# A gated recurrence with an FFT long convolution: gate factors made in float32r inside the scan, one batch ahead, and the filter's spectrum read from DRAM

## The chip, the cores and the metric

The kernel runs on one core of a Trainium2 chip. The metric is the device time of one execution in microseconds (us). TensorE (PE) multiplies, VectorE (DVE) and ScalarE (ACT) move and combine data, GpSimd (POOL) does elementwise work on SBUF, and SyncE (SP) issues the DMAs from one queue in order. Every engine runs its own instructions in their order and waits on semaphores for the others.

## The reference, cut to what matters

`B = 4`, `S = 6272`, `D = 256`. Two layers follow each other:

```python
sig = 1.0 / (1.0 + np.exp(-f_logit))
f = lower_bound + (1.0 - lower_bound) * sig
for t in range(S):                       # a gated scan over the sequence
    h = f[:, t] * h + (1 - f[:, t]) * x[:, t]
    y[:, t] = h
proj = y @ w_proj                        # 256 -> 768
x1, x2, x3 = proj[..., :D], proj[..., D:2*D], proj[..., 2*D:]
X2 = rfft(x2, n=S, axis=1); H = rfft(filter_fft, n=S, axis=0)
x2_conv = irfft(X2 * H, n=S, axis=1)     # circular convolution along the sequence
out = (x1 * x2_conv * x3) @ w_out
```

The length 6272 is split as 128 x 49, so that both transforms are matrix products.

## The kernel before, in words

For every batch `b` these stages follow each other:

- `hgrn(b)`: 13 chunks of 512 positions (the last has 128). A chunk loads `xt` and `ft` (512 KB each, `hg` pool, three buffers), takes the sigmoid on ACT (L139), multiplies on POOL (L140), and then, for each half `kh` of the 256 channels: four PE transposes of `ft` into bank 6 of PSUM (L146), four of `xt` into bank 7 (L148), an ACT pass that makes `fT` (L150) and the scan on DVE (L153). The scan reads bank 7 and writes the state as float16 into `HA`. Bank 6 and bank 7 have one copy each, so the second half's transposes wait for the first half's readers.
- `wraps()`: six DMAs inside `HA` that lay the state out periodically.
- `phase_p(b)`, `phase_f1(b)`: the product with the middle third of `w_proj` and the first transform; the result `A` overwrites the middle of `HA`.
- `mini(b)` and `units(b)`: 16 units. A unit makes two products of a transform matrix with `A` (L449, PSUM banks 0 and 1), multiplies each on DVE with the filter's spectrum `H`, which stays in SBUF (L453, into `PP`), transforms back with 16 products (L461, banks 2 and 3) and copies the result to `Th` on ACT (L464).
- `phase_z(b)`: 13 groups of 490 positions, each in two halves `jb`. For a half, `x1` (bank 4) and `x3` (bank 5) are made from `HA` with four float16 matmuls each (L408: two halves of the channels, each with the weight's high part `W13h` and its low part `W13l`); ACT scales `x1` into `x1s` (L413), DVE multiplies both into `z` (L414). Both inputs of L414 are read in the order `r m`, with a step of 49 floats, and `z` lies as `[.., r, m]`.
- `phase_o(b)`: 13 steps: 16 last products of the inverse transform (L481), DVE multiplies by `z` in place (L485), 16 products with `w_out` (L493), ACT copy (L497), DMA out.

In the main loop `units(b)`, `phase_z(b)` and `hgrn(b+1)` are stepped together; the last batch has only the first two. Before the loop, `prepare` (tables, weights, and the filter's transform) is woven with `hgrn(0)`: it rearranges the filter into a high part `f2h` (ACT, L316) and a low part `f2l` (DVE, L317), transforms it with three float16 matmuls for each of 128 column blocks (L325 to L327), and then per group of 8 blocks with four float32r matmuls of 512 columns (L338), whose result ACT writes to `H` (L340). `pair()` hands out four pairs of PSUM banks in turn.

The order of the instructions on each engine is not this program order: a scheduler sorts them by priority and by when it expects them to be ready, and the pools decide where waits for free buffers stand.

## Time and profile before

| what | value |
|---|---|
| time, median of 3 runs | 833.88 us (832.01 to 840.72) |
| the profiled execution's own time | 831.66 us |
| its span, first to last instruction | 830.0 us |
| PE busy, of the span | 697.1 us (84%) |
| DVE busy | 554.7 us (67%) |
| ACT busy | 400.5 us (48%) |
| POOL busy | 141.3 us (17%) |
| chain that ended last: PE, DVE, DMA | 39%, 23%, 10% of the span |

Busy PE time counts each matmul from its start to its modelled end, and matmuls overlap: a row `366` ns long may stand 0.21 us behind the one before it. So the start-to-start distance of rows says what PE work costs, and the busy sum does not. A row "x4" merges four instructions; the last number in brackets is idle time of the engine before the row, with what ended it.

### The profile page before, as it was taken

The numbers are of one execution on the slowest core, as the hardware profiler recorded it, in microseconds if no ns is written. First come the engines' busy times: TensorE is split into PE (matmuls) and PEld (weight loads), VectorE is DVE, ScalarE is ACT, GpSimd is POOL, SyncE is SP. The second block draws the span as 40 slices with busy tenths as digits, with TensorE's granted clock in tenths as the row PEclk, the third lists the DMA queues.
The fourth block names the chain that finished last, engine by engine and source line by source line (L and its number), as shares of the span: only waits on it lengthen the run. The fifth ranks groups of instructions, "written<-read, shape, count | busy, mean of one in ns | idle before, by whom it ended". The sixth has DMA issues, their size and how long they took to land.

```text
span 830.0 us, 14314 instructions
## 1 busy us (share of the span) xinstructions
PE 697.1 (84%) x5924; PEld 498.0 (60%) x5924; DVE 554.7 (67%) x587; ACT 400.5 (48%) x498; POOL 141.3 (17%) x157
## 2 busy tenths in 40 slices
...
GB/s 327 248 117 175 152 65 203 2 1 103 154 125 152 179 216 160 1 51 118 160 130 116 251 204 58 1 102 155 124 153 85 155 162 1 1 1 1 1 121 191
DMA packets 64672, 97.99 MB, mean 118 GB/s; under 512 B 3296, under 2 KB 54368, under 8 KB 63840
## 3 DMA queue, kind: packets, MB, share of 16 engines
...
## 4 chain that ended last, share of the span: by engine, by line
PE 39%; DVE 23%; DMA 10%; issue 8%; ACT 5%; POOL 1%; DVEq 0%; ACTq 0%; SPq 0%; POOLq 0%
PE PS L493 11%; DVE PP L453 8%; PE PS L461 8%; DMA ft<-in_f_logit_dram 7%; PE PS L408 7%; DVE z L414 6%; PE PS L369 5%; DVE z L485 4%; DVE HA L153 4%; PE PS L481 2%; ACT x1s L413 2%; DMA xt<-in_x_dram 2%; PE PS L146 2%; PE PS L148 1%; PE PS L384 1%
## 5 line engine op out<-in xcount | busy, mean ns | idle before, releaser
L408 PE MATMUL PS<-HA,W13h 128*128 128x490 f16 (+1 forms) x416 | 152.3, 366 | 17.6 <-DVE z L414 17.4
L408 PE MATMUL PS<-HA,W13l 128*128 128x490 f16 (+1 forms) x416 | 152.3, 366 | 0.0
L414 DVE TENSOR_TENSOR z<-PS,x1s 128x490 f16<-128x490 f32 (+1 forms) x104 | 100.7, 968 | 75.7 <-ACT x1s L413 38.0
L140 POOL TENSOR_TENSOR xt<-xt,ft 128x1024 f32<-128x1024 f32 (+1 forms) x52 | 116.4, 2238 | 204.0 <-DMA xt<-in_x_dram 115.7
L453 DVE TENSOR_TENSOR PP<-PS,H 98x1008 f16<-98x1008 f32 x128 | 149.2, 1197 | 1.9 <-PE PS L449 1.7
L153 DVE TENSOR_TENSOR_SCAN HA<-fT,HA,PS 128x512 f16<-128x512 f32 (+1 forms) x96 | 116.0, 1208 | 50.2 <-PE PS L148 29.8
L461 PEld LDWEIGHTS <-PP 98*128 98x128 f16 x1024 | 83.8, 97 | 71.7 <-issue 47.0
L150 ACT ACTIVATE fT<-PS,nomc 128x512 f32<-128x512 f32 (+1 forms) x104 | 68.8, 661 | 104.4 <-PE PS L146 55.9
L485 DVE TENSOR_TENSOR z<-PS,z 128x1024 f16<-128x1024 f32 (+1 forms) x52 | 58.2, 1158 | 87.5 <-PE PS L481 87.5
L493 PE MATMUL PS<-Woh,z 128*128 128x256 f16 x392 | 89.0, 276 | 21.6 <-DVE z L485 21.6
L461 PE MATMUL PS<-VB,PP 98*128 98x196 f16 x512 | 95.7, 248 | 3.7 <-DVE PP L453 3.6
L493 PEld LDWEIGHTS <-z 128*128 128x128 f16 x784 | 75.2, 99 | 35.2 <-DVE z L485 25.9
L464 ACT CAST Th<-PS 128x784 f16<-128x784 f32 x64 | 52.0, 812 | 77.1 <-PE PS L461 77.1
L497 ACT ACTIVATE osb<-PS 128x1024 f32<-128x1024 f32 (+1 forms) x52 | 50.4, 973 | 80.1 <-PE PS L493 73.4
L493 PE MATMUL PS<-Wol,z 128*128 128x256 f16 x392 | 88.6, 276 | 0.0
L413 ACT ACTIVATE x1s<-PS 128x490 f32<-128x490 f32 (+1 forms) x104 | 59.2, 569 | 51.9 <-PE PS L408 51.8
L139 ACT ACTIVATE ft<-ft 128x1024 f32<-128x1024 f32 (+1 forms) x52 | 52.7, 1014 | 63.0 <-DMA ft<-in_f_logit_dram 62.5
L461 PE MATMUL PS<-VA,PP 98*128 98x196 f16 x256 | 58.7, 246 | 27.0 <-DVE PP L453 25.0
...
L146 PE MATMUL PS<-iden,ft 128*128 128x128 f32 x392 | 63.7, 281 | 18.1 <-ACT ft L139 11.4
L148 PE MATMUL PS<-iden,xt 128*128 128x128 f32 x392 | 65.3, 288 | 13.0 <-DVE HA L153 6.7
L408 PEld LDWEIGHTS <-W13l 128*128 128x128 f16 x416 | 40.5, 97 | 58.3 <-issue 29.1
(120 smaller groups left out, 971.3 us busy)
## 6 DMA issues: line engine op xcount, KB each, us to landing
xt<-in_x_dram SPq DMA_DIRECT2D x48, 512.0 KB, 4.8
ft<-in_f_logit_dram SPq DMA_DIRECT2D x48, 512.0 KB, 3.9
out_dram<-osb SPq DMA_DIRECT2D x48, 512.0 KB, 2.6
...
HA<-HA SPq DMA_DIRECT2D x12, 512.0 KB, 5.1
...
```

The costliest lines, as they stand in the source:

```text
L140: nc.gpsimd.tensor_tensor(xt[:, 0:nb], xt[:, 0:nb], ft[:, 0:nb], op=AOP.mult)
L146: nc.tensor.transpose(sT[:, j * 128:(j + 1) * 128], ft[:, j, cols], iden[:])
L148: nc.tensor.transpose(uT[:, j * 128:(j + 1) * 128], xt[:, j, cols], iden[:])
L150: nc.scalar.activation(fT[:, 0:n], sT, AF.Identity, scale=nomc[:, kh:kh + 1], bias=1.0)
L153: nc.vector.tensor_tensor_scan(HA[:, h0:h0 + n], fT[:, 0:n], uT, 0.0 if c == 0 else HA[:, h0 - 1:h0], op0=AOP.mult, op1=AOP.add)
L408: nc.tensor.matmul(PS[:, 4 + i, 0:cn], w[:, kh, js], HA[:, h0:h0 + cn], start=(n == 0), stop=(n == 3))
L413: nc.scalar.activation(x1s[:, 0:cn], PS[:, 4, 0:cn], AF.Copy, scale=ZS)
L414: nc.vector.tensor_tensor(z[:, jb, :, m0:m0 + mn], PS[:, 5, 0:cn].rearrange("p (m r) -> p r m", r=Q), x1s[:, 0:cn].rearrange("p (m r) -> p ...
L453: nc.vector.tensor_tensor(P[:TB, o, :, :, 1:64], px.unsqueeze(1).broadcast_to([TB, 2, UE, 63]), hh, op=AOP.mult)
L461: nc.tensor.matmul(o, P[:TB, a, h, 2 * pr:2 * pr + 2, :], v[:TB], start=(n == 0), stop=(n == 3))
L485: nc.vector.tensor_tensor(zz, pc[:, :, 0:rn * 128].rearrange("p a (i m) -> p a i m", m=128), zz, op=AOP.mult)
L493: nc.tensor.matmul(po[:, i, :], z[:, kh, r0 + i, :], w[:, kh, :], start=(n == 0), stop=(n == 3))
```

## The change

- `phase_z` is gone. In `hgrn`, after both scans of a chunk, `x1` and `x3` of that chunk are made with `W13` in float32r (eight matmuls of up to 512 columns, new L164, instead of 16 of 490), still in banks 4 and 5, with `x1s` (new L167, one buffer) and the product `z` (new L168) in position order. `z` has two buffers, since it is now made while the batch before is still in use.
- The scan (still L153) writes a float32r tile `h` (two buffers for each half); a POOL copy (L158) puts it into `HA` as float16.
- `units` no longer finds `H` in SBUF: `prepare` writes it to 16 DRAM tiles (L350), and each unit loads its piece `Hu` (196 KB, two buffers) by a DMA on SP's queue (L431) and multiplies with it (L439).
- `phase_o` reads `z` at a step of 49 elements (98 bytes) and writes the product to a new tile `y` inside `PP` (L473).
- In `prepare` the filter is one float32r tile `f2` (copied by ACT and DVE in turn, L325 and L327) and transformed with one float32r matmul of 128 columns for each block (L334) instead of three; weights are loaded first, `pair()` uses two pairs of banks until `prepare` has ended.
- `units(b)` and `hgrn(b+1)` are woven evenly; the last batch has `units` alone.

```diff
@@ hgrn
+                h = hg.tile([128, CH], F32R, name="h", tag=f"h{kh}")
                 nc.vector.tensor_tensor_scan(
-                    HA[:, h0:h0 + n], fT[:, 0:n], uT,
-                    0.0 if c == 0 else HA[:, h0 - 1:h0], op0=AOP.mult, op1=AOP.add)
+                    h[:, 0:n], fT[:, 0:n], uT,
+                    0.0 if c == 0 else last[kh][:, CH - 1:CH].bitcast(F32),
+                    op0=AOP.mult, op1=AOP.add)
+                last[kh] = h
+                nc.gpsimd.tensor_copy(HA[:, HB[kh] + t0:HB[kh] + t0 + n],
+                                      h[:, 0:n].bitcast(F32))
+            for jb in range(2):
+                for i in range(2):
+                    js = slice(i * 256 + jb * 128, i * 256 + jb * 128 + 128)
+                    for kh in range(2):
+                        nc.tensor.matmul(PS[:, 4 + i, 0:n], W13[:, kh, js], last[kh][:, 0:n],
+                                         start=(kh == 0), stop=(kh == 1))
+                x1s = hg.tile([128, CH], F32, name="x1s", tag="x1s", bufs=1)
+                nc.scalar.activation(x1s[:, 0:n], PS[:, 4, 0:n], AF.Copy, scale=ZS)
+                nc.vector.tensor_tensor(z[:, jb, t0:t0 + n], PS[:, 5, 0:n], x1s[:, 0:n],
+                                        op=AOP.mult)
             yield
@@ prepare
-            nc.scalar.copy(dh, src)
-            nc.vector.tensor_tensor(dl, src, dh, op=AOP.subtract)
+            if r0 % 8:
+                nc.vector.tensor_copy(fv[:, :, :, r0:r0 + rn], src)
+            else:
+                nc.scalar.copy(fv[:, :, :, r0:r0 + rn], src)
...
-                nc.tensor.matmul(pa[:, i, :], f2h[:, cs], D1[:], start=True, stop=False)
-                nc.tensor.matmul(pa[:, i, :], f2l[:, cs], D1[:], start=False, stop=False)
-                nc.tensor.matmul(pa[:, i, :], f2h[:, cs], D1l[:], start=False, stop=True)
+                nc.tensor.matmul(pa[:TB, i, :], f2[:, c0:c0 + TB], D1r[:],
+                                 start=True, stop=True)
...
-            nc.scalar.activation(H[:TB, :, u, :], px[:TB], AF.Copy, scale=HS)
+            hw = hws[u % 4]
+            nc.scalar.activation(hw[:TB], px[:TB], AF.Copy, scale=HS)
+            nc.sync.dma_start(H[u][:], hw[:TB])
@@ units
+            Hu = cw.tile([128, 2, UE * 64], F16, name="Hu", tag="Hu")
+            nc.sync.dma_start(Hu[:TB], H[u][:])
...
-                hh = H[:TB, :, u, :].rearrange("p a (i k) -> p a i k", k=64)[:, :, :, 1:64]
+                hh = Hu[:TB].rearrange("p a (i k) -> p a i k", k=64)[:, :, :, 1:64]
@@ phase_o
+        z = zt[b % 2][:].rearrange("p k (m r) -> p k r m", r=Q)
...
-            zz = z[:, :, r0:r0 + rn, :]
+            y = PP[:, r0 // 4 % 4 // 2, r0 // 4 % 2].rearrange(
+                "p a i k -> p a (i k)").rearrange("p a (i m) -> p a i m", m=128)[:, :, 0:rn]
             nc.vector.tensor_tensor(
-                zz, pc[:, :, 0:rn * 128].rearrange("p a (i m) -> p a i m", m=128), zz,
-                op=AOP.mult)
+                y, pc[:, :, 0:rn * 128].rearrange("p a (i m) -> p a i m", m=128),
+                z[:, :, r0:r0 + rn, :], op=AOP.mult)
@@ main loop
-        gu, gz = units(b), phase_z(b)
-        gh = hgrn(b + 1) if b + 1 < B else iter(())
-        for step in range(NU):
-            next(gz, None)
-            next(gu)
-            if step >= 2:
-                next(gh, None)
-        for g in (gu, gz, gh):
-            run(g)
+        if b + 1 < B:
+            weave((units(b), NU), (hgrn(b + 1), NCHK))
+        else:
+            run(units(b))
```

How the order moves on the three engines that matter, in the middle of a stage in which units and scan run together (batch 2's units, batch 3's scan):

On DVE before, one round of one unit and one chunk is two unit products, two scans and two gate products, each kind in a block of its own.

```order
L453 TENSOR_TENSOR PP<-PS,H 98x16x63 x2
L153 SCALAR_TENSOR_TENSOR HA<-fT,HA,PS 128x512 x2
L414 TENSOR_TENSOR z<-PS,x1s 128x49x10 x2
L453 TENSOR_TENSOR PP<-PS,H 98x16x63 x2
L153 SCALAR_TENSOR_TENSOR HA<-fT,HA,PS 128x512 x2
```

On DVE now, in the same stage, scans and unit products alternate, and the gate products read 512 positions in order.

```order
L153 SCALAR_TENSOR_TENSOR h<-fT,h,PS 128x512
L439 TENSOR_TENSOR PP<-PS,Hu 98x16x63
L153 SCALAR_TENSOR_TENSOR h<-fT,h,PS 128x512
L439 TENSOR_TENSOR PP<-PS,Hu 98x16x63
L168 TENSOR_TENSOR z_100<-PS,x1s 128x512 x2
L153 SCALAR_TENSOR_TENSOR h<-fT,h,PS 128x512
L439 TENSOR_TENSOR PP<-PS,Hu 98x16x63
```

The round still has six instructions; a unit product now stands between the two scans of a chunk, and the gate products come after both.

On PE before, the gate matmuls (L408) need only the finished state in `HA`, so they fill the places where the next transposes or unit products would wait.

```order
L461 MATMUL PS<-VB,PP 128x196
L461 LDWEIGHTS PP
L461 MATMUL PS<-VA,PP 128x196
L461 LDWEIGHTS PP
L461 MATMUL PS<-VB,PP 128x196
L146 MATMUL PS<-iden,ft 128x128 x4
L408 LDWEIGHTS W13h
L408 MATMUL PS<-HA,W13h 128x490
L408 LDWEIGHTS W13l
L408 MATMUL PS<-HA,W13l 128x490
L461 LDWEIGHTS PP
L461 MATMUL PS<-VB,PP 128x196
```

On PE now, at the same place, the gate matmuls (L164; their weight load is part of the instruction) stand around the transposes of the next chunk.

```order
L447 MATMUL PS<-VA,PP 128x196
L447 LDWEIGHTS PP
L447 MATMUL PS<-VB,PP 128x196
L146 MATMUL PS<-iden,ft 128x128 x3
L164 MATMUL PS<-h,W_73 128x512 x2
L146 MATMUL PS<-iden,ft 128x128
L148 MATMUL PS<-iden,xt 128x128 x3
L164 MATMUL PS<-h,W_73 128x512 x2
L447 LDWEIGHTS PP
L447 MATMUL PS<-VB,PP 128x196
```

The first L164 pair waits for the second scan of its own chunk, and the second pair for ACT's `x1s` of the first half; what stands behind them waits too.

On SP before, the queue holds only the chunk loads and now and then a wrap.

```order
L135 DMA xt<-in_x_dram 128x4x256
L137 DMA ft<-in_f_logit_dram 128x4x256
L160 DMA HA<-HA 128x2048
L135 DMA xt<-in_x_dram 128x4x256
L137 DMA ft<-in_f_logit_dram 128x4x256
L135 DMA xt<-in_x_dram 128x4x256
L162 DMA HA<-HA 128x1920
```

On SP now, a load of `Hu` stands between the chunk loads.

```order
L137 DMA ft<-in_f_logit_dram 128x4x256
L431 DMA Hu<-H_91 98x1024
L135 DMA xt<-in_x_dram 128x4x256
L431 DMA Hu<-H_92 98x1024
L137 DMA ft<-in_f_logit_dram 128x4x256
L135 DMA xt<-in_x_dram 128x4x256
L431 DMA Hu<-H_93 98x1024
```

Each `Hu` is issued only after the chunk load ahead of it has got its buffer.

## Rows read from the trace of the kernel before

**Rows 1.** Windows, batches 1 and 3: length; PE, PEld, DVE, ACT, POOL busy; clock; DMA.

```profile
347.14:467.25 120.11, 105.84 (x745) 68.47 (x744) 91.77 (x89) 54.91 (x80) 28.16 (x28) 1.00 0.40 126
700.62:790.37 89.75, 82.26 (x551) 46.18 (x550) 63.03 (x64) 26.45 (x42) 3.95 (x16) 1.00 0.00 1
```

**Rows 2.** Timeline of DVE in batch 1's stage: start us, us, instruction, idle before.

```profile
389.43 2.31 DVE L453 TENSOR_TENSOR PP<-PS,H 98x1008 f16<-98x1008 f32 x2
391.66 1.27 DVE L153 TENSOR_TENSOR_SCAN HA<-fT,HA,PS 128x512 f16<-128x512 f32 x1
393.75 1.28 DVE L153 TENSOR_TENSOR_SCAN HA<-fT,HA,PS 128x512 f16<-128x512 f32 x1 [0.82 <-PE PS L148]
...
397.30 1.00 DVE L414 TENSOR_TENSOR z<-PS,x1s 128x490 f16<-128x490 f32 x1 [1.40 <-ACT x1s L413]
...
433.42 2.31 DVE L453 TENSOR_TENSOR PP<-PS,H 98x1008 f16<-98x1008 f32 x2
```

**Rows 3.** Timeline of PE in the same stage.

```profile
399.90 0.60 PE L146 MATMUL PS<-iden,ft 128*128 128x128 f32 x4
400.93 0.25 PE L461 MATMUL PS<-VA,PP 98*128 98x196 f16 x1
401.01 0.33 PE L461 MATMUL PS<-VB,PP 98*128 98x196 f16 x2
402.48 0.37 PE L408 MATMUL PS<-HA,W13h 128*128 128x490 f16 x1
402.69 0.37 PE L408 MATMUL PS<-HA,W13l 128*128 128x490 f16 x1
```

**Rows 4.** Timeline of PE in the filter's transform.

```profile
127.36 2.09 PE L338 MATMUL PS<-af,FTr 98*98 98x512 f32 x8 [1.13 <-ACT af L331]
129.47 0.22 PE L325 MATMUL PS<-D,f2h 128*128 128x128 f16 x1
129.53 0.22 PE L326 MATMUL PS<-D,f2l 128*128 128x128 f16 x1
```

**Rows 5.** Groups by line: instructions, busy us, mean ns, idle before.

```profile
L414 DVE TENSOR_TENSOR z<-PS,x1s 128x490 f16<-128x490 f32 (+1 forms) x104 | 100.7, 968 | 75.7 <-ACT x1s L413 38.0 <-PE PS L408 31.6 <-PE PS L449 3.3
L413 ACT ACTIVATE x1s<-PS 128x490 f32<-128x490 f32 (+1 forms) x104 | 59.2, 569 | 51.9 <-PE PS L408 51.8
L430 DVE TENSOR_TENSOR pb<-PS,Hm 98x512 f16<-98x512 f32 x8 | 5.2, 686 | 2.4 <-PE PS L408 1.9 <-PE PS L425 0.5
L373 DVE CAST x<-PS 128x1024 f16<-128x1024 f32 x24 | 34.5, 1444 | 20.2 <-PE PS L369 20.2
L388 DVE CAST HA<-PS 98x1024 f16<-98x1024 f32 x32 | 36.6, 1216 | 4.2 <-PE PS L384 4.2
L317 DVE TENSOR_TENSOR f2l<-PS,f2h 128x1024 f16<-128x1024 f32 (+1 forms) x13 | 19.9, 1533 | 5.4 <-ACT f2h L316 5.4
```

**Rows 6.** Timeline of DVE: batch 3's last units, which run alone, and the stage's end.

```profile
783.36 2.32 DVE L453 TENSOR_TENSOR PP<-PS,H 98x1008 f16<-98x1008 f32 x2 [0.60 <-PE PS L449]
786.27 1.21 DVE L453 TENSOR_TENSOR PP<-PS,H 98x1008 f16<-98x1008 f32 x1 [0.60 <-PE PS L449]
790.37 2.36 DVE L485 TENSOR_TENSOR z<-PS,z 128x1024 f16<-128x1024 f32 x2 [2.88 <-PE PS L481]
```

**Rows 7.** DMA issues: KB each, median us to landing.

```profile
ft<-in_f_logit_dram SPq DMA_DIRECT2D x48, 512.0 KB, 3.9
ft<-in_f_logit_dram SPq DMA_DIRECT2D x4, 128.0 KB, 2.0
```

**Rows 8.** Waits of SP's queue in batch 1's stage: us in total, times, longest.

```profile
SPq L137 <- PE PS L146: 99.1, 12, 36.5
```

**Rows 9.** Windows: the filter's rearrangement and its transform, both beside `hgrn(0)`.

```profile
24.00:66.00 42.00, 27.02 (x130) 19.96 (x130) 38.68 (x57) 33.73 (x37) 12.80 (x13) 0.94 0.50 165
72.00:140.00 68.00, 58.36 (x569) 46.30 (x570) 29.11 (x25) 39.48 (x47) 17.16 (x24) 0.95 0.39 121
```

**Rows 10.** Windows just after the start of `phase_o(3)`.

```profile
791.00:794.00 3.00, 2.35 (x12) 1.63 (x13) 1.72 (x2) 0.00 (x0) 0.00 (x0) 0.61 0.00 0
```

More of the change, by code (lines that the diff above doesn't have):

```diff
@@ L110 @@
     HB = (0, S + EW)
-    PP = konst.tile([128, 2, 2, 2, UE, 64], F16, name="PP")
     raws = [HA[:, S + 4096 * k:S + 4096 * (k + 1)].bitcast(F32)
-            .rearrange("m (r d) -> m r d", d=D) for k in range(4)]
+            .rearrange("m (r d) -> m r d", d=D) for k in range(3)]
+    hws = [HA[:, S + 12288 + 1024 * k:S + 12288 + 1024 * (k + 1)]
+           .rearrange("p (a n) -> p a n", a=2) for k in range(4)]
     hg = ctx.enter_context(tc.tile_pool(name="hg", bufs=2))
-    cv = ctx.enter_context(tc.tile_pool(name="cv", bufs=1))
+    dram = ctx.enter_context(tc.tile_pool(name="dram", bufs=1, space=bass.MemoryType.DRAM))
+    H = [dram.tile([TB, 2, UE * 64], F16, name=f"H{u}") for u in range(NU)]
+    zt = [konst.tile([128, 2, S], F16, name="z0"), None]
     psp = ctx.enter_context(tc.tile_pool(name="psp", bufs=1, space=PSUM))
     PS = psp.tile([128, 8, 512], F32, name="PS")
-    turn = [0]
+    turn = [0, 2]
     def pair():
-        turn[0] = (turn[0] + 1) % 4
+        turn[0] = (turn[0] + 1) % turn[1]
         return PS[:, 2 * turn[0]:2 * turn[0] + 2]
     def hgrn(b):
+        z = zt[b % 2]
+        last = [None, None]
         for c in range(NCHK):
@@ L171, in prepare @@
                                 op0=AOP.mult, op1=AOP.add)
+        wp = raws[0][:, 0:6].rearrange("p a d -> p (a d)").rearrange("p (k j) -> p k j", k=2)
+        nc.sync.dma_start(wp, moe_w_proj.rearrange("(a p) j -> p a j", p=128))
+        wo = raws[1][:, 0:2]
+        nc.sync.dma_start(wo, moe_w_out.rearrange("(a p) j -> p a j", p=128))
+        for kh in range(2):
+            nc.vector.tensor_scalar(wp[:, kh, :], in0=wp[:, kh, :], scalar1=omc[:, kh:kh + 1],
+                                    scalar2=None, op0=AOP.mult)
+            for i, j0 in enumerate((0, 512)):
+                dst = slice(i * 256, (i + 1) * 256)
+                nc.vector.tensor_copy(W13[:, kh, dst], wp[:, kh, j0:j0 + 256])
+            for p in range(2):
+                nc.vector.tensor_copy(
+                    W2[:, kh].rearrange("k (g p e) -> k p e g", p=2, e=2)[:, p],
+                    wp[:, kh, 256 + p * 128:256 + (p + 1) * 128]
+                    .rearrange("k (e g) -> k e g", e=2))
+        nc.vector.tensor_copy(Woh[:], wo[:])
+        nc.vector.tensor_tensor(Wol[:], wo[:], Woh[:], op=AOP.subtract)
+        yield
         def icol(pattern, base, cm, n, name):
```

85 lines of the change are left out of this document (18 added, 67 removed).

## The prediction

> **What bounds the kernel now.** I read the granted clock first (full in these stages, a little less in `prepare` [rows 1, 9]), then windows by stage, then the DVE and PE timelines inside a stage, and last the DMA and queue views. More than half of the span lies in four stages in which a batch's units run. In batch 1's it is 120.1 us, in batch 3's, which has no scan beside it, 89.8 us [rows 1]; batches 0 and 2 have a scan beside them as batch 1 does. PE is busiest in both, but its rows overlap, so I price it by distances: an L408 of 490 columns starts 0.21 us after the one before, so an L449 of 512 costs 0.22; a second L461 adds 0.08 us; four transposes take 0.60 us less a tail of 0.17 [rows 3]. One round of a unit and a chunk then needs on PE 16 x 0.21 (L408) + 16 x 0.08 (L461) + 4 x 0.22 (L449) + 4 x 0.43 (L146, L148) = 7.2 us. The round itself is (433.42 - 389.43) / 5 = 8.80 us [rows 2]. On DVE it has two L453 (2.31 together), two scans of 1.27 and two L414 of 0.97: 6.8 us [rows 2, 5], and DVE waits, up to 1.4 us at a time, for `x1s`, which waits for PE [rows 2]. So PE's work plus a handful of hand-overs sets the round; DVE is close behind.
>
> **The gate factors in the scan, beside units (batches 0 to 2).** 16 L408 go, 8 float32r matmuls of 512 columns come. The nearest row is L338, float32r with 512 columns: eight in 2.09 us less a tail of 0.2, or 0.24 each [rows 4]. PE's round falls from 7.2 to 7.2 - 3.36 + 1.92 = 5.8 us. On DVE, L414 (0.97 for 490, both inputs read at a step of 49 floats) becomes L168, 512 in order, for which L430 is the nearest row: 0.69 [rows 5]. DVE's round falls to 2.31 + 2.54 + 1.38 = 6.2 us, so DVE now has the larger sum. But the new order has a chain, and I walked it by hand with these durations. First scan ends at 0; the unit's first product runs to 1.15; the second scan to 2.42; PE's first gate matmuls end at 2.95; ACT's `x1s` (0.57 [rows 5]) at 3.5; DVE does the unit's second product to 3.58 and `z` of the first half to 4.3; PE can write bank 4 again at 3.6 and bank 5 at 4.3, so `z` of the second half runs from about 5.0 to 5.7; PE, held by these waits, reaches the next chunk's transposes for the scan at about 5.6, and the next first scan ends at 7.1. With the last transposes' hand-over I take **7.2 us**. Ends: 6.2 (DVE without any wait) and 8.0 (half of the 1.6 us won is lost to the queueing behind L164). There are 12.25 full chunks in a stage (6272 / 512), the rest of it (start, spare units, end) I leave: 12.25 x (8.8 - 7.2) = 19.6, times three: **-58.8 us** (ends -95 and -29).
>
> POOL gets 26 copies a stage. No row shows a copy of this shape; POOL's 28 instructions there take 28.2 of 120 us [rows 1], so even at 2 us each they fit beside the rest, at no cost. If POOL were full, the scans would wait for a free `h`.
>
> **The last batch.** Its 13 gate groups vanish. Units alone already stand in the trace: 786.27 - 783.36 = 2.91 us each, and 4.1 us from the last unit's first product to `phase_o` [rows 6]. The new stage is 15 x 2.91 + 4.1 + about 2.2 for `mini` (two L430 of 0.69 [rows 5], and its two adds, estimated at a bit more than one L430) = 50.0 us against 89.8 [rows 1]: **-39.7 us**.
>
> **The spectrum from DRAM.** 64 loads of 196 KB, between the 2.0 us of a 128 KB load and the 3.9 of 512 KB [rows 7]; by size 2.4, plus 0.5 to issue and hand over. The buffer is free when the second product of the unit two earlier ends; in the units-alone stage the next use comes 2 x 2.91 - 2.32 = 3.5 us later [rows 6], in a 7.2 us round far later. So 2.9 is hidden and I take nothing; at 3.9 + 0.5 a unit would take 3.36 us, +6 us in all.
>
> **`phase_o`.** L485 becomes L473, which reads `z` at a step of 98 bytes. Two steps make a round, and their two products stand together (2.36 us [rows 6]): PE has to wait for the first, while the second hides behind the first's L493. L414, with both inputs strided, costs 0.97 where 490 elements in order would cost about 0.66 by L430: 0.31 more, or 0.63 ns per element. L373 against L388 shows a strided PSUM read (with a strided write) at 0.22 ns per element [rows 5]. I give the difference, 0.41 to 0.5 ns, to the strided SBUF read: +0.5 us for 1024 elements, once per round, 6.5 rounds, four batches: **+13 us**. Ends: 0 (no penalty) and +21 (0.65 us, and the second product just too late). The Trainium skill (SBUF — State Buffer, section "Door 1: The DMA port swizzle") says that SBUF is read in lines of 16 bytes and that each access that goes to a new line pays; by that rule every element of this read pays, which speaks against this edit, but no run of before shows such a float16 read on DVE.
>
> **`prepare`.** The filter's rearrangement keeps DVE busy for 38.7 of 42 us [rows 9]. Twelve L317 of 1.53 [rows 5] become about six copies of 1.44 (as L373), saving about 9.7, and five chunks' gate products cost 10 x 0.69 = 6.9: about even. In the transform two groups of blocks and a chunk make a round, PE's part of which was 48 x 0.06 (L325 to L327) + 8 x 0.24 + 16 x 0.11 = 6.4 [rows 3, 4]. Now 16 L334: no row shows float32r with 128 columns; below, a float32 weight of 128 columns every 0.11 (the transposes), above, 0.24 as for 512 columns. I take 0.11, since the weights are the transposes' size: 1.8 + 1.9 + 1.8 + 1.9 (gates) = 7.4, so +1.0 a round, and eight rounds: +8 (with 0.24: +24). The filter's first megabyte is now loaded ahead of the first chunk, which delays it by less than the 3.9 us that 512 KB take alone to land [rows 7], since loads overlap: +2, an estimate. Together **+10 us** (0 to +26).
>
> **Sum.** 830.0 - 58.8 - 39.7 + 13 + 10 = 754.5 us of span. The profiled run's own time was 1.7 above its span and the median 2.2 above that: **758 us**.
>
> **Rivals.**
>
> (a) DVE saturates: rounds of 6.2, the chain hidden by the order. 36 us less: about 722. For it: PE and ACT have room. Against: the walk shows two waits in each round that no other work fills. Chance 0.10.
> (b) The extras cost their upper ends and the round is 8.0: 758 + 29 + 16 + 8 = about 811. For it: in the new PE order the gate matmuls wait for their own chunk's scan, while L408 never did; two PSUM pairs instead of four in `prepare`. Chance 0.14.
> (c) The clock falls in the last stage, where units run alone. PE's 2.1 us per unit would double, to about 5 us per unit: +33, 791 us. For it: just after the units-alone stretch the clock was 0.61 for 3 us [rows 10]. Against: over the stage up to there it was 1.00 [rows 1]. Chance 0.06.
> (d) Slower: SP's queue exposes `Hu`. SP stood 99 of 120 us waiting to issue `ft` [rows 8], and `Hu` now stands behind such an issue. If the `ft` ahead of it waits for transposes that stand on PE behind a product that needs this `Hu`, each round pays its whole load, 2.9 us: 758 + 48 x 2.9 = 897. It decides from (830 - 754.5) / 48 = 1.6 us per unit of these three stages on. Against: the `ft` that waits was for a chunk three ahead, and a `Hu` has a whole round to land. Chance 0.04.
> (e) The round stays at 8.8, since the scan's own chain of transposes, `fT` and scan set it and not PE: 758 + 59 = 817. Against: DVE idles longer for `x1s` (1.40), which is behind PE's gate matmuls, than for the scan's transposes (0.82) [rows 2]. Chance 0.06.
>
> **How the numbers follow.** My forecast has 0.60: 758, its own range 738 to 778 (round 6.8 to 7.6, 15 either way, the strided read and `prepare` 10 more). The range of 8 in 10 reaches down to half of (a) and up into (b) and (c): 730 to 797. About 1% is what a measurement of this kernel can tell from no change. Faster by more than that are the forecast, (a), (b), (c) and (e), less the corners where two of them meet: 0.91; slower: (d) and what joins it, 0.05; within 1%: 0.04.
>
> **What would show it.** Rounds in the DVE timeline of batch 1's stage: 7.2 us, with L164 at 0.24 and L168 at 0.69. Batch 3's stage: 50 us, units 2.9 apart, no idle put down to the DMA of `Hu`. L473 at 1.7 us, rounds of `phase_o` half a microsecond longer. `prepare` with its scan ends about 10 us later than now; L334 0.11 apart. The forecast is wrong if rounds stay near 8.8, if DVE waits for `Hu`, or if L164 costs two passes, 0.43 us.

## The result and the profile after

The changed kernel takes 787.4 us (median of four runs, 786.4 to 791.0) against 834.2 for the kernel before on the same chip: a ratio of 0.943, 95% interval 0.937 to 0.950. The forecast was 758 with a range of 730 to 797, so the time lies inside the range, but above the forecast's own range of 738 to 778: the change gained 47 us where 76 were worked out. The profiled execution has a span of 785.2 us, 44.8 less than before.

Windows of the changed kernel: length; busy PE, PEld, DVE, ACT, POOL with instructions; granted clock; DMA share; GB/s. The first is everything up to the first unit, then come the stages of batches 0 to 3, then `phase_o(1)` and `phase_o(3)`; the last fence is `phase_o(1)` of before.

```profile
0.00:173.10 173.10, 135.51 (x826) 107.35 (x826) 109.91 (x177) 113.73 (x143) 60.07 (x83) 0.93 0.54 175
173.10:275.54 102.44, 92.97 (x646) 64.36 (x646) 84.15 (x88) 53.92 (x81) 44.70 (x54) 0.99 0.59 188
343.42:450.79 107.37, 93.27 (x644) 63.84 (x644) 84.32 (x90) 54.22 (x81) 46.76 (x55) 0.99 0.57 179
519.73:619.73 100.00, 91.01 (x639) 62.79 (x639) 84.12 (x89) 51.73 (x78) 39.74 (x52) 1.00 0.50 161
687.85:735.13 47.28, 41.91 (x340) 29.60 (x342) 38.60 (x37) 12.99 (x16) 3.99 (x16) 0.92 0.22 60
450.79:497.20 46.41, 33.48 (x376) 25.62 (x372) 28.19 (x13) 12.04 (x12) 0.25 (x1) 0.88 0.32 128
735.13:785.20 50.07, 32.88 (x376) 25.11 (x370) 28.35 (x13) 12.68 (x13) 0.00 (x0) 0.90 0.32 129
```

```profile
467.25:501.20 33.95, 28.71 (x382) 24.18 (x377) 14.58 (x14) 13.12 (x13) 4.66 (x2) 1.00 0.51 198
```

Against before, stretch by stretch (a stage is counted from the end of the last copy of `phase_f1`, L388 before and L398 now, to the first product of `phase_o`):

| stretch | before | after | difference | forecast |
|---|---|---|---|---|
| up to the first unit (`prepare`, first `phase_p`, `phase_f1`) | 169.2 | 173.1 | +3.9 | +10 |
| units beside a scan, batches 0, 1, 2 | 122.3, 120.0, 121.8 | 102.4, 107.4, 100.0 | -54.3 | -58.8 |
| batch 3's stage | 89.8 | 47.3 | -42.5 | -39.7 |
| four `phase_o` | 141.5 | 187.4 | +45.9 | +13 |
| the rest (`phase_p` and `phase_f1` of batches 1 to 3) | 65.5 | 67.6 | +2.1 | 0 |
| span | 830.0 | 785.2 | -44.8 | -75.5 |

The stages did nearly what was forecast. One row is far off: `phase_o`, 33 us above its forecast, and the span as a whole is 31 above its own; the other rows nearly cancel.

DVE in batch 1's stage, one round (start us, us, instruction, idle before): 388.02 to 395.43 is 7.41 us, where [rows 2] showed 8.80 on average.

```profile
388.02 1.28 DVE L153 TENSOR_TENSOR_SCAN h<-fT,h,PS 128x512 fp32r<-128x512 f32 x1 [0.18 <-PE PS L148]
389.22 1.18 DVE L439 TENSOR_TENSOR PP<-PS,Hu 98x1008 f16<-98x1008 f32 x1
390.32 1.27 DVE L153 TENSOR_TENSOR_SCAN h<-fT,h,PS 128x512 fp32r<-128x512 f32 x1
391.50 1.18 DVE L439 TENSOR_TENSOR PP<-PS,Hu 98x1008 f16<-98x1008 f32 x1
392.81 0.69 DVE L168 TENSOR_TENSOR z<-PS,x1s 128x512 f16<-128x512 f32 x1
394.82 0.69 DVE L168 TENSOR_TENSOR z<-PS,x1s 128x512 f16<-128x512 f32 x1 [1.32 <-ACT x1s L167]
395.43 1.27 DVE L153 TENSOR_TENSOR_SCAN h<-fT,h,PS 128x512 fp32r<-128x512 f32 x1
```

DVE in `phase_o(1)`: two full steps (L473) take 4.60 us where L485 took 2.36 [rows 6], and a round is 7.18 us.

```profile
474.24 4.60 DVE L473 TENSOR_TENSOR PP<-PS,z 128x1024 f16<-128x1024 f32 x2 [2.58 <-PE PS L468]
481.42 4.60 DVE L473 TENSOR_TENSOR PP<-PS,z 128x1024 f16<-128x1024 f32 x2 [2.58 <-PE PS L468]
```

PE in the same round: after the inverse transform (L468) it waits for the first L473, runs its 16 output products (L481), and waits again for the second.

```profile
473.81 0.84 PE L468 MATMUL PS<-ID,Th 64*128 64x128 f16 x24
476.63 0.28 PE L481 MATMUL PS<-Woh,PP 128*128 128x256 f16 x1 [1.98 <-DVE PP L473]
...
478.90 0.28 PE L481 MATMUL PS<-Woh,PP 128*128 128x256 f16 x1 [0.35 <-DVE PP L473]
```

The page sums it up (groups by line: busy us, mean ns, idle before): PE stood 53.7 us for L473.

```profile
L473 DVE TENSOR_TENSOR PP<-PS,z 128x1024 f16<-128x1024 f32 (+1 forms) x52 | 113.4, 2220 | 76.0 <-PE PS L468 56.4
L481 PE MATMUL PS<-Woh,PP 128*128 128x256 f16 x392 | 101.8, 299 | 54.0 <-DVE PP L473 53.7
```

**Theory.** The order of work in `phase_o` was right; the price of the read at a step of 98 bytes was mis-sized: L473 takes 2.3 us for 1024 elements, not 1.74. **Rivals:** the new write into `PP` or its reuse makes L473 long; or the stages, the `Hu` loads or the filter hide losses that only seem small.

### The profile page after: what moved, and what is told of

It reads as the page before. It is cut to its first block, busy times and chain, and to the rows that moved or that the text cites. A ratio compares the mean times of both kernels' runs of the same rounds, so it can differ in the third digit from the quotient of the medians.

```text
span 785.2 us, 13221 instructions
## 1 busy us (share of the span) xinstructions
PE 645.1 (82%) x5252; PEld 483.2 (62%) x5252; DVE 567.9 (72%) x574; ACT 390.1 (50%) x495; POOL 198.4 (25%) x264
## 4 chain that ended last, share of the span: by engine, by line
PE 36%; DVE 22%; issue 13%; ACT 8%; DMA 8%; POOL 0%; DVEq 0%; ACTq 0%; SPq 0%; POOLq 0%
PE PS L481 8%; DVE PP L473 8%; PE PS L164 7%; DVE h L153 7%; PE PS L379 5%; PE PS L447 5%; DVE PP L439 5%; DMA ft<-in_f_logit_dram 4%; DMA Hu<-H 4%; PE PS L468 2%; PE PS L394 2%; PE PS L148 2%; PE PS L346 2%; PE PS L435 2%; ACT x1s L167 1%
## 5 line engine op out<-in xcount | busy, mean ns | idle before, releaser
L473 DVE TENSOR_TENSOR PP<-PS,z 128x1024 f16<-128x1024 f32 (+1 forms) x52 | 113.4, 2220 | 76.0 <-PE PS L468 56.4
L164 PE MATMUL PS<-h,W 128*128 128x512 f32 (+1 forms) x416 | 148.9, 443 | 17.5 <-DVE h L153 10.7
L439 DVE TENSOR_TENSOR PP<-PS,Hu 98x1008 f16<-98x1008 f32 x128 | 151.2, 1194 | 9.6 <-PE PS L435 3.4
L481 PE MATMUL PS<-Woh,PP 128*128 128x256 f16 x392 | 101.8, 299 | 54.0 <-DVE PP L473 53.7
L140 POOL TENSOR_TENSOR xt<-xt,ft 128x1024 f32<-128x1024 f32 (+1 forms) x52 | 116.6, 2243 | 101.7 <-DMA xt<-in_x_dram 54.8
L153 DVE TENSOR_TENSOR_SCAN h<-fT,h,PS 128x512 fp32r<-128x512 f32 (+1 forms) x96 | 116.0, 1208 | 23.4 <-ACT fT L150 7.9
L481 PEld LDWEIGHTS <-PP 128*128 128x128 f16 x784 | 79.7, 106 | 78.9 <-DVE PP L473 63.4
L485 ACT ACTIVATE osb<-PS 128x1024 f32<-128x1024 f32 (+1 forms) x52 | 50.7, 975 | 139.6 <-PE PS L481 139.6
L168 DVE TENSOR_TENSOR z<-PS,x1s 128x512 f16<-128x512 f32 (+1 forms) x104 | 68.3, 657 | 59.2 <-ACT x1s L167 37.2
L158 POOL CAST HA<-h 128x512 f16<-128x512 f32 (+1 forms) x104 | 61.6, 594 | 170.8 <-DVE h L153 167.6
L481 PE MATMUL PS<-Wol,PP 128*128 128x256 f16 x392 | 101.1, 297 | 0.0
L164 PEld LDWEIGHTS PS<-h,W 128*128 128x128 f32 x416 | 66.2, 195 | 43.7 <-DVE h L153 24.6
L167 ACT ACTIVATE x1s<-PS 128x512 f32<-128x512 f32 (+1 forms) x104 | 59.3, 571 | 66.6 <-PE PS L164 62.9
L435 PE MATMUL PS<-HA,FT 98*128 98x512 f16 x256 | 77.7, 386 | 4.6 <-DVE PP L439 2.8
```

The costliest lines, as they stand in the source:

```text
L140: nc.gpsimd.tensor_tensor(xt[:, 0:nb], xt[:, 0:nb], ft[:, 0:nb], op=AOP.mult)
L153: nc.vector.tensor_tensor_scan(h[:, 0:n], fT[:, 0:n], uT, 0.0 if c == 0 else last[kh][:, CH - 1:CH].bitcast(F32), op0=AOP.mult, op1=AOP.add)
L164: nc.tensor.matmul(PS[:, 4 + i, 0:n], W13[:, kh, js], last[kh][:, 0:n], start=(kh == 0), stop=(kh == 1))
L168: nc.vector.tensor_tensor(z[:, jb, t0:t0 + n], PS[:, 5, 0:n], x1s[:, 0:n], op=AOP.mult)
L435: nc.tensor.matmul(PS[:, o, :], FT[:TB, tb, :], A[:TB, es, r, :], start=(n == 0), stop=(n == 1))
L439: nc.vector.tensor_tensor(P[:TB, o, :, :, 1:64], px.unsqueeze(1).broadcast_to([TB, 2, UE, 63]), hh, op=AOP.mult)
```

## The experiments

All ratios are to the kernel before, run on the same chip; the changed kernel's is 0.943.

### Is it the step of the read? Reading `z` in order

```diff
-        z = zt[b % 2][:].rearrange("p k (m r) -> p k r m", r=Q)
+        z = zt[b % 2][:].rearrange("p k (r m) -> p k r m", r=Q)
```

> phase_o reads z in the order in which it lies in SBUF (so each step multiplies with the wrong positions of z; all else is unchanged, same element counts and same write into y). Theory, the 98-byte step of the read of z is what makes L473 2.33 us: L473 falls to the 1.24 us of L485 before, the round of two steps from 7.2 to about 5.6, the three inner phase_o from 45.4 to about 34, the last from 50.1 to 40, granted clock there back to 1.00, total 787 - 45 = 742. Rival, the new write into y in PP, or the wait for its reuse, costs it: L473 stays at 2.3 and the total at 787.

This kernel leaves out the right order of `z`; its counts are the same. 742.1 us, ratio 0.889 (0.886 to 0.893). Group by line, then DVE's rounds of 5.55 us in `phase_o(2)`, then its window:

```profile
L473 DVE TENSOR_TENSOR PP<-PS,z 128x1024 f16<-128x1024 f32 x48 | 56.5, 1220 | 71.1 <-PE PS L468 51.8 <-issue 19.1
```

```profile
607.31 2.36 DVE L473 TENSOR_TENSOR PP<-PS,z 128x1024 f16<-128x1024 f32 x2 [3.19 <-PE PS L468]
612.86 2.36 DVE L473 TENSOR_TENSOR PP<-PS,z 128x1024 f16<-128x1024 f32 x2 [3.19 <-PE PS L468]
```

```profile
596.16:629.60 33.44, 28.27 (x376) 23.82 (x375) 14.58 (x14) 11.88 (x12) 0.24 (x1) 1.00 0.40 165
```

The same count, the same PSUM operand and the same write into `y`, read in order, cost what L485 cost, and 45 us come back, as expected. The write into `PP` and its reuse are not the cause. The granted clock of the four `phase_o` is 0.95 to 1.00 again (0.88 to 0.93 after the change). In the changed kernel's `phase_o(1)` it stood at half (0.50) from 448 to 458, after PE had been busy for only 0.6 of the 4 us from 444 to 448, at the end of the stage, and near half (0.57) once more from 492 to 496, after four rounds in which PE waited for L473; the second kind of spell is gone with the read in order.

### What a step costs

```diff
+        steps = (1, 2, 3, 4, 6, 8, 12, 16, 24, 32, 48, 49, 49)
...
-                z[:, :, r0:r0 + rn, :], op=AOP.mult)
+                zv, op=AOP.mult)
```

> A price list: the thirteen steps of each phase_o read z with steps of 1, 2, 3, 4, 6, 8, 12, 16, 24, 32, 48, 49 and 49 elements of two bytes (wrong positions of z; the count, the PSUM read and the write into y stay). The known ends are 1.22 us (step 1) and 2.33 us (step 49) for 1024 elements. Theory A, lines of 16 bytes as the Trainium skill has them (SBUF — State Buffer, Door 1: The DMA port swizzle: at least two accesses must fall into a line): 1.22 up to a step of 4, and 2.33 from 8 on. Theory B, every step other than 1 pays in full: 2.33 from step 2 on. Theory C, only steps that are not a multiple of four bytes pay (49 is odd): 2.33 at 3 and 49 alone.

A single run, 764.6 us, which leaves out the right positions of `z`; what counts are the rows. `zv` is `z` read with the step of that turn. DVE in `phase_o(0)`: steps 3 and 4 in one row, then 6, 8, 12, 16, 24, 32, 48 and 49 elements (1 and 2 together took 2.36 us as well).

```profile
284.71 2.36 DVE L482 TENSOR_TENSOR PP<-PS,z 128x1024 f16<-128x1024 f32 x2 [5.54 <-issue]
290.26 1.51 DVE L482 TENSOR_TENSOR PP<-PS,z 128x1024 f16<-128x1024 f32 x1 [3.19 <-PE PS L469]
291.69 1.98 DVE L482 TENSOR_TENSOR PP<-PS,z 128x1024 f16<-128x1024 f32 x1
296.25 1.94 DVE L482 TENSOR_TENSOR PP<-PS,z 128x1024 f16<-128x1024 f32 x1 [2.58 <-PE PS L469]
298.11 1.99 DVE L482 TENSOR_TENSOR PP<-PS,z 128x1024 f16<-128x1024 f32 x1
302.68 1.93 DVE L482 TENSOR_TENSOR PP<-PS,z 128x1024 f16<-128x1024 f32 x1 [2.58 <-PE PS L469]
304.53 1.89 DVE L482 TENSOR_TENSOR PP<-PS,z 128x1024 f16<-128x1024 f32 x1
308.99 2.70 DVE L482 TENSOR_TENSOR PP<-PS,z 128x1024 f16<-128x1024 f32 x1 [2.58 <-PE PS L469]
311.62 2.34 DVE L482 TENSOR_TENSOR PP<-PS,z 128x1024 f16<-128x1024 f32 x1
```

Up to 8 bytes nothing is paid, at 12 bytes 0.3 us, from 16 to 64 bytes 0.7, and at 96 and 98 bytes 1.5 and 1.1. Theories B and C fall, and theory A holds only for where the price begins, not for one full price from there on. The Trainium skill (SBUF — State Buffer, section "Door 1: The DMA port swizzle") asks for at least two accesses in a line of 16 bytes: where the price begins agrees with that. The figure it draws from it, eight bf16 elements as the reach that is free, does not: a step of eight two-byte elements cost 0.7 us here. The second rise, beyond 64 bytes, is not in the rule, and its cause stays open.

### Can the order of the elements be chosen better?

Four ways to have the same data meet `y` in a better order. First, L473 with the four neighbours of `z` innermost:

```diff
-                y, pc[:, :, 0:rn * 128].rearrange("p a (i m) -> p a i m", m=128),
-                z[:, :, r0:r0 + rn, :], op=AOP.mult)
+                y.rearrange("p a i m -> p a m i"),
+                pc[:, :, 0:rn * 128].rearrange("p a (i m) -> p a m i", m=128),
+                z[:, :, r0:r0 + rn, :].rearrange("p a r m -> p a m r"), op=AOP.mult)
```

> Same data, but L473 goes through its elements with the four positions that lie side by side in z innermost (8 bytes in a row, then a jump of 98), and therefore reads PSUM in steps of 512 bytes and writes y in steps of 256. Theory, the price hangs on how often the SBUF read jumps: 1024 elements with 256 jumps, about 1.45 us (as L373, 1024 elements written in runs of four, 1.44): rounds of 5.9, total about 750. Rival, any operand with a large step costs two cycles per element, PSUM or the write too: L473 stays at 2.3 or more, total 787 or more.

930.9 us, ratio 1.115 (1.110 to 1.121): L473 takes 4.8 us. The read of `z` jumps four times less often, but the write now jumps 256 bytes for each element, and the PSUM read 512. The next two kernels write at the same step, with PSUM read in order or not at all, and pay the same price per element, so the write alone is enough to explain it.

```profile
L473 DVE TENSOR_TENSOR PP<-PS,z 128x1024 f16<-128x1024 f32 x48 | 222.2, 4815 | 89.2 <-PE PS L468 71.1 <-issue 18.0
```

Second and third, `z` is stored as `[r, m]` when it is made, and read in order. L168 itself writes it so, in three pieces a half (the rest of a row of 49, whole rows, the start of a row):

```diff
+                zr = z[:].rearrange("p k (r m) -> p k m r", r=Q)
+                for p0, p1 in rows(t0, t0 + n):
...
+                    nc.vector.tensor_tensor(
+                        zr[:, jb, m:m + mn, r:r + rn],
+                        PS[:, 5, p0 - t0:p1 - t0].rearrange("p (m r) -> p m r", r=rn),
+                        x1s[:, p0 - t0:p1 - t0].rearrange("p (m r) -> p m r", r=rn),
+                        op=AOP.mult)
```

Or L168 writes a small tile `zs` in position order, and POOL copies the same pieces:

```diff
+                nc.gpsimd.tensor_copy(
+                    zr[:, :, m:m + mn, r:r + rn],
+                    zs[:, :, p0 - t0:p1 - t0].rearrange("p k (m r) -> p k m r", r=rn))
```

> L168 itself writes z in the order r, m: three instructions for each half of a chunk, a write with a step of 256 bytes, both reads in order; phase_o reads z in the order in which it lies. Theory, a strided write costs DVE as the strided read does, 2.2 ns per element: 512 x 2.2 = 1.13 and two short pieces of 0.1 to 0.2 in place of 0.66, +0.8 for each half, rounds of 7.35 + 1.6 = 8.9, stages +60, phase_o -45: about 800. Rival, a strided write is cheap and only reads pay: +0.3 for each half, rounds of 7.9, +21 - 45: about 763.

> L168 writes a small tile in position order, POOL copies each chunk of it into z in the order r, m (three copies for each chunk: the rest of a row of 49, whole rows, the start of a row), and phase_o reads z in the order in which it lies, as before the change. Theory: phase_o as with the read in order (-45 us), POOL has room (44.7 of 102 us busy in a stage; the copies add 13 times about 1.2 to 2.5 us, 16 to 32), so the stages stay at 100 to 107: about 742. Rival: the copies take more than POOL's free time, or hold up L158 and L140 on POOL in front of the scan, and the rounds grow from 7.3 to 8.5 or more: 3 x 12 x 1.2 = 43 us given back, 785.

By DVE: 868.5 us, ratio 1.041 (1.038 to 1.043); by POOL: 783.7, 0.940 (0.938 to 0.942). `phase_o` gained as expected in both, but a two-byte write at a step of 256 bytes costs 4.7 to 4.8 ns per element on either engine, twice the strided read, so both theories missed, and DVE's version its rival too. First fence DVE's L178, second POOL's L181 (groups by line and shape), then POOL's version in batch 1's stage, in which POOL is busy 100.6 of 116.7 us:

```profile
L178 DVE TENSOR_TENSOR z<-PS,x1s 128x490 f16<-128x490 f32 x48 | 112.7, 2349 | 5.3 <-PE PS L170 2.2 <-ACT x1s L173 2.2 <-PE PS L460 0.9
```

```profile
L181 POOL COPY z<-zs 128x980 f16<-128x980 f16 x24 | 110.9, 4620 | 2.7 <-DVE zs L175 2.7
```

```profile
358.64:475.31 116.67, 95.53 (x644) 65.90 (x644) 84.25 (x90) 54.47 (x81) 100.58 (x92) 0.93 0.53 165
```

The rival of the POOL version held: its copies fill POOL, which the scan's L140 and L158 also need. The three stages take 332 us where they took 310, and the first unit begins at 190.9 in place of 173.1; together they give back what `phase_o` gains. Fourth, chunks of ten whole rows, so that runs of ten can be written; the reorder is then a strided read, by PE from `h`, or by DVE from PSUM and `x1s` as L414 did:

```diff
-CH = 512
+CH = 490
...
-                        nc.tensor.matmul(PS[:, 4 + i, 0:n], W13[:, kh, js], last[kh][:, 0:n],
+                        nc.tensor.matmul(PS[:, 4 + i, 0:n], W13[:, kh, js], last[kh][:, 0:n]
+                                         .rearrange("p (m r) -> p r m", r=Q),
```

Or, with the matmul left as it was:

```diff
+                nc.vector.tensor_tensor(
+                    zr[:, jb, :, m0:m0 + mn],
+                    PS[:, 5, 0:n].rearrange("p (m r) -> p r m", r=Q),
+                    x1s[:, 0:n].rearrange("p (m r) -> p r m", r=Q), op=AOP.mult)
```

> Chunks of 490 positions (ten rows of 49, five blocks of 98 for the transposes) in place of 512; the gate matmuls read the state h with a step of 49 floats, so that x1 and x3 stand in PSUM in the order r, m; L168 reads in order and writes z as [r, m] in runs of ten; phase_o reads z in the order in which it lies. Theory: phase_o back to 34 us (-45); L168 stays under 0.8; the step of the moving operand costs PE nothing, or up to 0.2 per matmul (8 x 0.2 x 36 = +58). POOL's L140 and ACT's sigmoid work on 1280 elements in place of 1024 (+0.55 and +0.2 a chunk, beside other work). About 745 if the step is free, 800 if it costs 0.2.

> As rows490_pe, but the gate matmuls read h in order and L168 reads PSUM and x1s with a step of 49 floats, as L414 did before the change, writing runs of ten. Theory: L168 goes from 0.69 to the 0.97 of L414, +0.56 a round of DVE, of which PE waits for at most half in the round (PE sets it): +10 to +20; phase_o -45: 755 to 765. Rival: the chunk's form (98 partitions, five blocks) costs more than phase_o gains, 787.

By PE: 788.8 us, ratio 0.948 (0.943 to 0.953); by DVE: 762.3, 0.915 (0.913 to 0.918). Groups by line: L164 with PE's strided read and, in the other kernel, in order; then DVE's strided read:

```profile
L164 PE MATMUL PS<-h,W 128*128 128x490 f32 (+1 forms) x416 | 232.2, 651 | 6.8 <-DVE h L153 2.8 <-ACT x1s L168 2.2 <-DVE z L171 1.0
L164 PE MATMUL PS<-h,W 128*128 128x490 f32 (+1 forms) x416 | 153.1, 447 | 21.2 <-DVE h L153 9.4 <-ACT x1s L167 4.8 <-DVE z L170 4.7
```

```profile
L170 DVE TENSOR_TENSOR z<-PS,x1s 128x490 f16<-128x490 f32 (+1 forms) x104 | 104.2, 1002 | 49.5 <-ACT x1s L167 37.0 <-PE PS L164 8.7 <-PE PS L451 1.2
```

A step of 196 bytes in the moving operand makes each gate matmul of the same chunk 0.2 us longer (651 against 447 ns), the upper end of what was expected, and PE has no room for it. DVE's strided read costs 1.00 us, near the 0.97 of L414 [rows 5], and fits: its stages are 104 to 106 us. Of the 24 us by which its span lies above that of the reading in order (`o_seq`), 10 stand ahead of the first unit, which begins at 185.9 in place of 175.5, and 9 in the three stages; which part of the new chunk's form costs this was not taken apart.

### POOL gathers `z` in `phase_o`

```diff
+            zc = cw.tile([128, 2, 4, 128], F16, name="zc", tag="zc", bufs=3)
+            nc.gpsimd.tensor_copy(zc[:, :, 0:rn], z[:, :, r0:r0 + rn, :])
...
-                z[:, :, r0:r0 + rn, :], op=AOP.mult)
+                zc[:, :, 0:rn], op=AOP.mult)
```

> POOL, which stands idle in phase_o, copies the four rows of z that a step needs into a small tile (three buffers) ahead of L473, with the read in steps of 98 bytes on POOL and a write in order; L473 then reads in order. Theory: L473 back to 1.22 us and rounds of 5.55, as long as two copies of POOL fit into a round (each under 2.8 us): about 742 + 2 = 745. POOL's strided writes took 4.7 ns per element; if its strided reads cost half of that, 2.4 us a copy, it just fits. Rival: a copy takes 3.5 us or more, POOL becomes the bound of phase_o: 13 copies x 3.5 = 45 us per phase, no gain, 787 or more.

745.0 us, ratio 0.895 (0.890 to 0.901): 5% less than the changed kernel and the fastest kernel of this study that leaves nothing out. POOL's timeline in `phase_o(2)` (two copies 4.73 us), then DVE's (rounds of 5.62):

```profile
611.21 4.73 POOL L461 COPY zc<-z 128x1024 f16<-128x1024 f16 x2 [0.84 <-DVE PP L475]
616.83 4.73 POOL L461 COPY zc<-z 128x1024 f16<-128x1024 f16 x2 [0.88 <-DVE PP L475]
```

```profile
609.92 2.36 DVE L475 TENSOR_TENSOR PP<-PS,zc 128x1024 f16<-128x1024 f32 x2 [3.25 <-issue]
615.54 2.36 DVE L475 TENSOR_TENSOR PP<-PS,zc 128x1024 f16<-128x1024 f32 x2 [3.26 <-PE PS L470]
```

The strided read costs POOL about as much as it cost DVE (2.37 us), but POOL has nothing else to do there and the copies run ahead of PE's wait.

### What made the stages shorter: float32r, or the new place?

The gates with two float16 weights from `HA`, at the new place:

```diff
-                        nc.tensor.matmul(PS[:, 4 + i, 0:n], W13[:, kh, js], last[kh][:, 0:n],
-                                         start=(kh == 0), stop=(kh == 1))
+                        h0 = HB[kh] + t0
+                        for w in (W13h, W13l):
+                            nc.tensor.matmul(PS[:, 4 + i, 0:n], w[:, kh, js], HA[:, h0:h0 + n],
```

And the float32r matmuls issued twice:

```diff
-                for i in range(2):
+                for i in (0, 0, 1, 1):
```

> The gates are made with float16 weights in a high and a low part from the float16 state in HA, as before the change (16 matmuls a chunk at 0.21 in place of 8 at 0.24), but at the changed kernel's place, inside hgrn in position order; all else is as in the changed kernel. Theory, PE's own work sets the round and float32r's saving of 3.4 - 1.9 = 1.5 us is the whole of the step from 8.80 to 7.35: rounds of 8.85, three stages +55 in sum, hgrn(0) in prepare +12 to +18, total 787 + 70 = 857. Rival, most of the gain came from the new place and the reads in order, and the chain, not PE's sum, sets the round: at most +25, 812.

> Every gate matmul (L164) is issued twice, the second time over the first's result; all else is as in the changed kernel. It adds 8 x 0.24 = 1.9 us of PE work to each round. Theory, PE's own work sets the round of 7.35 us (it is the sum of PE's parts, 7.2): rounds of 9.2, three stages +70, hgrn(0) in prepare +10 to +20 at most: about 787 + 80 = 867. Rival, the round is set by the chain transposes, fT, scan, gates, x1s, L168 and PE has slack: half of the added work or less shows, +35 at most, 825.

856.4 us, ratio 1.030 (1.027 to 1.034), and 868.4, ratio 1.042 (1.039 to 1.044). The stages of batches 0 to 2, float16 first, then twice float32r:

```profile
194.39:314.71 120.32, 109.52 (x749) 69.08 (x750) 84.55 (x89) 55.47 (x81) 45.14 (x54) 1.00 0.50 155
381.84:501.78 119.94, 109.09 (x749) 68.93 (x749) 84.51 (x89) 55.70 (x81) 45.19 (x54) 1.00 0.49 154
568.87:688.70 119.83, 108.71 (x739) 68.37 (x738) 84.48 (x88) 53.32 (x78) 40.53 (x52) 1.00 0.42 133
```

```profile
189.58:314.87 125.29, 115.35 (x744) 82.64 (x745) 84.71 (x89) 55.73 (x81) 45.31 (x54) 1.00 0.51 154
383.20:508.84 125.64, 116.04 (x757) 82.90 (x755) 84.32 (x89) 56.13 (x81) 45.16 (x54) 1.00 0.49 151
577.08:702.14 125.06, 115.37 (x745) 82.24 (x745) 84.28 (x88) 53.36 (x78) 40.65 (x52) 1.00 0.41 129
```

With float16 the three stages take 360.1 us, against 364.1 before the change and 309.8 after: in them the new place alone is worth 4 us, float32r 50. Doubling the gates lengthens the stages by 66 us, 1.7 for each of 39 chunks where 1.9 were added. PE's busy time in the three stages is 277 us in the changed kernel, 327 with float16 gates and 347 with doubled ones, and what is left of their lengths, 33, 33 and 29, hardly moves: PE's work enters the stages nearly one for one. The float16 gates also wait for POOL's copy into `HA`; with PE idle for the same 33 us that wait does not explain the 50. With float16 gates the change is slower than the kernel before.

### The loads of `Hu`, and the filter

```diff
-            Hu = cw.tile([128, 2, UE * 64], F16, name="Hu", tag="Hu")
-            nc.sync.dma_start(Hu[:TB], H[u][:])
+            if u < 2:
+                Hu = cw.tile([128, 2, UE * 64], F16, name="Hu", tag=f"Hu{u}", bufs=1)
+                nc.sync.dma_start(Hu[:TB], H[u][:])
+                st[f"Hu{u}"] = Hu
+            Hu = st[f"Hu{u % 2}"]
```

And, in another kernel, the filter as `f2h` and `f2l`:

```diff
-                nc.tensor.matmul(pa[:TB, i, :], f2[:, c0:c0 + TB], D1r[:],
-                                 start=True, stop=True)
+                nc.tensor.matmul(pa[:, i, :], f2h[:, cs], D1[:], start=True, stop=False)
+                nc.tensor.matmul(pa[:, i, :], f2l[:, cs], D1[:], start=False, stop=False)
+                nc.tensor.matmul(pa[:, i, :], f2h[:, cs], D1l[:], start=False, stop=True)
```

> Only the first two pieces of the filter's spectrum are loaded in each batch and used for all 16 units (so 14 of 16 units multiply with the wrong piece); the other 56 loads of 196 KB are gone from SP's queue and from the DMA engines. Theory, the loads are hidden (2.8 us of waits for Hu in the whole trace of the changed kernel): 787 stays, at most 3 to 6 less, and most of that in the last batch's stage, where the units stand alone. Rival, SP's order and the DMA traffic hold up the loads of ft and xt in front of the transposes without showing as waits for Hu: stages of 95 in place of 100 to 107, about 765 to 770.

> The filter is kept as two float16 tiles again (high part by ACT, low part by DVE) and transformed with three float16 matmuls for each block, as before the change; all else is as in the changed kernel. By the prediction's steps the float32r filter was even in the rearrangement and lost 1.0 us in each of eight rounds of the transform, so undoing it would give 8 back: 779. By the trace of the changed kernel, prepare got only 4 us longer, with POOL's new copies, the gate matmuls of batch 0 and the weights loaded first in it, so the float32r filter should itself have gained: undoing it loses 5 to 15, 792 to 802.

The first kernel leaves out 56 of the 64 loads: 782.9 us, ratio 0.939 (0.933 to 0.944). The interval overlaps that of the changed kernel, and the stages of the profiled execution are 102.4, 104.3, 100.0 and 48.9 against 102.4, 107.4, 100.0 and 47.3: at most a few microseconds, as the theory had it. The changed kernel's page gives `Hu` 4% of the chain that ended last, 31 us: a share of that chain is not what taking the transfer away would gain. With the float16 filter 801.7 us, ratio 0.962 (0.956 to 0.967); it stands ahead of the first unit, which begins at 189.2 where it was 173.1. The first of the two expectations, 779, fell; it charges the filter with a microsecond a round that the prediction's sum puts on the gates (see `prepare` below). PE in the filter's transform of the changed kernel (eight float32r matmuls in 0.83 us), and DVE's pass over the filter's low part in the kernel with the float16 filter:

```profile
97.41 0.83 PE L334 MATMUL PS<-D1r,f 128*98 128x128 f32 x8
```

```profile
L330 DVE TENSOR_TENSOR f2l<-PS,f2h 128x1024 f16<-128x1024 f32 (+1 forms) x13 | 19.7, 1529 | 2.3 <-ACT f2h L329 2.3
```

## Why the prediction was right in direction and 29 us too low

- **`phase_o`, +13 forecast, +46 measured: the step that failed.** The prediction split L414's 0.63 ns of extra per element between PSUM and SBUF and gave the strided read 0.5 us for 1024 elements, L473 1.74 us; its upper end was 0.65. The read costs 1.1 us. At 1.74 the second product would just have hidden, as the prediction had it; at 2.33 it does not. The wait for the first product and the part of the second that no longer hides give (2.33 - 1.24) + (2.33 - 1.76) = 1.66 us a round (the 1.76 being the sixteen L481 that cover the second), and 7.18 - 5.55 = 1.63 was measured; over 26 rounds that is 42 of the 46 us. Longer rounds at half the clock add to it: the first of `phase_o(1)` takes 9.12. The row it was drawn from was the wrong kind: L414 steps over four-byte elements, 490 at a time, and its price was divided over two operands; why two-byte elements pay more is not shown. The price list has 0.3 to 0.7 for steps of 12 to 64 bytes, where 0.5 would have been near. That the time still lies inside 730 to 797 is luck as far as this term goes: the upper part of that range was there for rivals (b) and (c), in which this read is 8 us at most. The Trainium skill's rule of lines (SBUF — State Buffer, section "Door 1: The DMA port swizzle"), set beside this term and not priced, pointed the right way.
- **Stages of batches 0 to 2, -58.8 forecast, -54.3 measured: right in size, and only in part for the reason given.** L168 takes 0.69 as forecast, and DVE waits for the second `x1s` as in the walk. But the prediction put PE's work at 5.8 us of a round of 7.2, below DVE's 6.2, and laid the rest on a chain of hand-overs; the two gate kernels show that work added on PE lengthens the stages nearly one for one, so PE had no such room. The float32r matmuls stand 0.28 apart and not 0.24 (PE's rows below: two in 0.57 us; in the doubled kernel's runs of six it is 0.25), 0.3 more for eight, about what a round of 7.4 has over 7.2. Rival (a), rounds of 6.2, and rival (e), 8.8, fell; of rival (b) only the strided read came, and it went past its upper end.

```profile
391.64 0.73 PE L164 MATMUL PS<-h,W 128*128 128x512 f32 x2
392.21 0.27 PE L146 MATMUL PS<-iden,ft 128*128 128x128 f32 x1
```

- **One stage stays longer, not foreseen.** Batch 1's is 5 to 7 us above its neighbours. ACT's timeline at its end (the changed kernel): the sigmoid of a chunk of the next batch waits for its `ft`, and the last `Th` and `x1s` copies stand behind it in order. No run here was made to take this wait alone away; without the loads of `Hu` it is still there (3.52 us, with the stage at 104.3), so they do not cause it.

```profile
446.65 1.06 ACT L139 ACTIVATE ft<-ft 128x1024 f32<-128x1024 f32 x1 [4.28 <-DMA ft<-in_f_logit_dram]
447.61 0.80 ACT L450 CAST Th<-PS 128x784 f16<-128x784 f32 x1
448.30 0.28 ACT L167 ACTIVATE x1s<-PS 128x128 f32<-128x128 f32 x1
```

- **Last stage, -39.7 forecast, -42.5 measured: right.** The granted clock was 0.92 over it, where rival (c) had PE at half speed: that rival fell.
- **`Hu`, 0 forecast: right.** In the whole trace DVE waits 2.8 us for it (its group below); without the loads nothing clear is gained. Rival (d) fell.

```profile
L439 DVE TENSOR_TENSOR PP<-PS,Hu 98x1008 f16<-98x1008 f32 x128 | 151.2, 1194 | 9.6 <-PE PS L435 3.4 <-DMA Hu<-H 2.8 <-PE PS L447 2.3
```

- **`prepare`, +10 forecast, +4 measured: near, by the steps given.** The prediction's terms for the float32r filter are 9.7 us less in the rearrangement and about 1 less in each of eight rounds of the transform (16 matmuls at 0.11 for 48 at 0.06), some 17 in all; for the rest of the change they are 6.9 and eight times 1.9 for the gates, and 2 for the loads, some 24. With the float16 filter the first unit begins at 189.2, 20 later than before the change: that is the rest; the float32r filter then takes 16 out. The 779 in the expectation above counted the gates' 1.9 a round against the filter. L334 stands (0.83 - 0.22) / 7 = 0.087 us apart, below the lower bound of 0.11, and a copy of the filter takes DVE 1.24 us and not 1.44; the pass of DVE over the low part that is gone is 1.5 us long, 13 times. One sum in the prediction is off: as its factors stand, the old round of the transform adds up to 6.6 and not 6.4 us, so the new one is 0.8 longer and not 1.0.
- **Sum.** Of the 31 us that the span lies above the forecast of 754.5, `phase_o` has +33, the stages +4.5, the stretches between +2; the last stage (-3) and `prepare` (-6) go the other way.
